# Every fifth broadcast of source indices on eight DMA engines instead of sixteen

## The chip, the cores and the metric

The kernel runs on one core of one Trainium2 chip. What counts is the device time of one execution in microseconds (us), as the median over several runs. A profile is one further execution, taken by the hardware profiler; its span runs from the first to the last instruction of the program.

Engines are named as in the profile: PE is the matrix engine, PEld its weight load, DVE the vector engine, ACT the scalar engine, POOL the GpSimd engine and SP the engine whose queue issues most of the plain transfers. Transfers are carried out by 16 DMA engines; a queue (q0, q1, q10 and so on) is a list of transfers that several DMA engines work on.

## What is computed

One layer of mean aggregation over a graph of 12,500 nodes and 800,000 edges, with 64 features a node:

```python
def reference(x, src, dst, deg_inv, w_self, w_neigh):
    N = x.shape[0]
    nsum = _segment_sum(x[src], dst, N)        # sum of x[src] over the edges of each dst
    h_neigh = nsum * deg_inv[:, None]
    return x @ w_self + h_neigh @ w_neigh
```

`src` and `dst` are random node numbers, so both the gather `x[src]` and the sum by `dst` are irregular.

## The kernel before

The irregular part is turned into matrix products. The edges are packed into 32-bit keys, sorted in runs of 6250 a partition, merged, and so brought into 8526 buckets. A bucket holds the edges whose destination lies in one block of 144 nodes and whose source lies in one block of 128 nodes; it has at most 128 edges (64 for each half of the destination block). All of this takes about the first half of the time.

For each bucket two lists of small numbers are left. One says which row of the destination block an edge goes to; it stays on the chip, transposed, in the tile `dlT`. The other says which of the 128 rows of the source block an edge takes. It is written to device memory as `sl`, one row of 128 numbers (bf16, 256 bytes) for a bucket.

The second half of the time is the loop in `nodes`, which walks through the buckets in tiles of 8. Its steps are:

- `one_hots` makes the operands for 28 buckets at a time, 305 times in all. Line 777, on SP's queue, fetches 28 rows of `sl`, that is 3584 numbers or 7168 bytes, and writes the same 7168 bytes to each of the 128 partitions of the tile `slb`: this is the broadcast that the change is about, 896 KB written for each. `slb` has three buffers. Line 779, on DVE, compares `slb` with the partition's own number and so makes the one-hot tile `ohs` (source row by edge; three buffers). Line 782, on DVE too, makes the one-hot tile `ohd` (edge by destination row; six buffers) from `dlT`.
- `gather` multiplies, on PE, each bucket's `ohs` with the rows of `x` of its source block (line 807, into the PSUM tile `ct`, 8 buckets each). ACT (line 817), and later sometimes DVE (line 815), copies `ct` to `xg`.
- `sums` multiplies `xg` with `ohd` and adds up in PSUM (line 863, tiles `acc`).
- Every 7 destination blocks, `finish` multiplies the sums with `w_neigh`, scales, adds the self term and stores the output.

The order of all this is written out by hand (`manual_schedule`), and each engine's queue runs in that order. `gather` asks `one_hots` for the next 28 buckets as soon as fewer than 44 buckets beyond its own 8 are ready (`AHEAD`), so one-hots are made a group or two ahead of the products. SP issues the broadcast of a group once DVE has read the `slb` buffer three groups back (line 779). Between the groups, DVE runs the merge of the second part of the keys (`merge_round`, lines 280 and 292) in the first part of the loop, and smaller work later. Other transfers in the loop are gathers and stores on POOL's queue (`v`, `lx`, `sl`, `out`), loads and stores on ACT's queue (`fo`, one store of merged rows `d`), and the fetching of instructions.

Of the kernel before, what the change touches and what calls it, by code (L numbers as in the profile page):

```python
# [335 lines left out]
class Kernel:  # L336
# [433 lines left out]
    def one_hots(self, pool):  # L770


        nc = self.nc
        for c in range(0, NBID, 28):
            b = pool.tile([128, 28 * 128], BF, name="slb", bufs=3)
            src = self.sl[c:c + 28]
            nc.sync.dma_start(b, bass.AP(tensor=src.tensor, offset=src.offset, ap=[[0, 128], [1, 28 * 128]]))
            s = pool.tile([128, 28, 128], FH, name="ohs", bufs=3)
            nc.vector.tensor_scalar(s.rearrange("p c s -> p (c s)"), b, self.pidx[:, :1], None, op0=OP.is_equal)  # L779
            d = pool.tile([128, 14, HN, 2], FH, name="ohd", bufs=6)  # L780
            ix = self.dlT[:, c:c + 28].rearrange("p (c t) -> p c t", t=2)[:, :, None, :].to_broadcast([128, 14, HN, 2])
            nc.vector.tensor_tensor(d, self.iota[:, None].to_broadcast([128, 14, HN, 2]), ix, op=OP.is_equal)  # L782
            yield [(s[:, j], d[:, j // 2, :, j % 2]) for j in range(28)]
# [376 lines left out]
```

## Time and profile before

| | |
|---|---|
| Time, median of 3 runs | 2198.76 us |
| The three runs | 2186.39, 2199.57, 2198.76 us |
| Time of the profiled execution | 2187.6 us |
| Span of the profiled execution | 2185.9 us |
| Busy in the span: PE, DVE, ACT, POOL | 1026.7, 1997.1, 1263.6, 648.6 us |
| Broadcasts on line 777 | 305, issued from 1098.1 to 2160.9 us |
| Moved by the DMA engines | 331.46 MB, of it 299.80 MB on q1 (SP's queue) |

The busy time of an engine is the time in which it executes; the profile also tells, for each stretch in which an engine was idle, what it had been waiting for. For the DMA engines the profile gives, by queue, the number of packets, the bytes, and the time that the packets took as a share of the time of all 16 engines; it does not say which engine carried which packet. The share and the bytes of a queue together give the pace of one engine while it works for that queue. All views can be cut to a stretch of the span, given in us from its start.

### The profile page before, as it was taken

Reading aid. Unit: us, or ns where it says so; the run is one execution under the profiler, and the core shown is the slowest. Engines: PE = TensorE matmul, PEld = TensorE weight load, DVE = VectorE, ACT = ScalarE, POOL = GpSimd, SP = SyncE. Lnnn points to the kernel's source line nnn. Section 1 sums busy time; section 2 is a strip of 40 time slices with the busy share of each in tenths; the row PEclk is TensorE's granted clock in tenths of the full one; section 3 lists DMA queues with packets and bytes.
Section 4 is the critical chain, followed back from the end, with each engine's and each line's share of the span. In section 5 each row is a group of like instructions: output and inputs, shape, how many; then the busy total and the mean of one; then the engine's idle time right before and its main releaser. Section 6 shows DMA issues by size and latency. Waiting matters only on the chain.

```text
span 2185.9 us, 59793 instructions
## 1 busy us (share of the span) xinstructions
PE 1026.7 (47%) x26089; PEld 885.7 (41%) x26089; DVE 1997.1 (91%) x2193; ACT 1263.6 (58%) x1743; POOL 648.6 (30%) x1016
## 2 busy tenths in 40 slices
PE   0050000000000000000068998999987989999888
PEld 0050000000000000000067887878776877788777
DVE  7899999999899599988999999999998988898887
ACT  6470000009700000062269999999998888898887
POOL 0000000000888888977771101011340110100110
PEclk9975555555555555555589999999999999999999
DMA  5140000001000000011177787777876787787785
GB/s 162 29 107 11 0 0 0 0 7 53 21 20 19 18 13 14 10 50 51 47 271 263 269 293 265 280 262 281 309 275 232 274 288 281 264 312 280 272 284 177
DMA packets 111471, 331.46 MB, mean 152 GB/s; under 512 B 57008, under 2 KB 65136, under 8 KB 110560
## 3 DMA queue, kind: packets, MB, share of 16 engines
q1 hardware_dynamic: 74127, 299.80, 37.0%
q0 software_dynamic: 14736, 18.99, 4.9%
q10 hardware_dynamic: 22337, 8.76, 1.8%
q8 instruction: 206, 3.38, 0.6%
q14 instruction: 65, 0.53, 0.1%
HBM read 308.39 MB, written 19.10 MB: 150 GB/s over the span
## 4 chain that ended last, share of the span: by engine, by line
PE 36%; DVE 33%; POOL 10%; issue 9%; ACT 8%; DMA 2%; ACTq 1%; another core or an unknown queue 0%; DVEq 0%; POOLq 0%; SPq 0%
PE ct L807 21%; PE acc L863 14%; DVE a L228 9%; DVE b L228 9%; POOL u L467 6%; DVE u L292 6%; ACT xg L817 3%; POOL pad L382 2%; ACT junka L448 2%; DVE u L324 2%; DMA v<-d,ix 1%; POOL v L625 1%; PE po L931 1%; DVE u L280 1%; ACT junk L604 1%
## 5 line engine op out<-in xcount | busy, mean ns | idle before, releaser
L817 ACT ACTIVATE xg<-ct 128x1024 f16<-128x1024 f32 (+1 forms) x994 | 939.1, 1091 | 99.2 <-PE ct L807 79.1
L807 PE MATMUL ct<-xh,ohs 128*128 128x128 f16 x8526 | 600.7, 221 | 58.0 <-issue 24.6
L807 PEld LDWEIGHTS <-ohs 128*128 128x128 f16 x8526 | 496.5, 99 | 104.7 <-issue 44.1
L467 POOL DMA_INDIRECT u<-d,ix x256 | 336.0, 1313 | 543.4 <-ACT junka L448 500.8
L292 DVE TENSOR_TENSOR u<-u 128x256 f32<-128x256 f32 (+47 forms) x494 | 452.8, 947 | 23.1 <-ACT u L276 15.7
L863 PE MATMUL acc<-ohd,xg 64*128 64x72 f16 x17052 | 410.1, 194 | 49.2 <-issue 35.1
L863 PEld LDWEIGHTS <-xg 64*128 64x128 f16 x17052 | 323.9, 94 | 124.6 <-issue 45.7
L779 DVE TENSOR_SCALAR ohs<-slb,pidx 128x3584 f16<-128x3584 bf16 x305 | 350.1, 1148 | 20.3 <-PE ct L807 17.1
L782 DVE TENSOR_TENSOR ohd<-iota,dlT 128x2016 f16<-128x2016 bf16 x305 | 365.8, 1199 | 0.0
L692 PE MATMUL tr<-idb,l 128*128 128x128 bf16 x68 | 9.0, 271 | 492.5 <-ACT l L686 487.6
L228 DVE TENSOR_TENSOR b<-a 128x106 f32<-128x106 f32 (+36 forms) x112 | 227.3, 2080 | 10.3 <-ACT a L231 9.3
L228 DVE TENSOR_TENSOR a<-b 128x106 f32<-128x106 f32 (+31 forms) x114 | 228.5, 2056 | 1.2
L276 ACT ACTIVATE u<-u 128x256 f32<-128x256 f32 (+15 forms) x94 | 47.3, 589 | 309.7 <-DVE u L280 308.3
L692 PEld LDWEIGHTS <-l 128*128 128x128 bf16 x68 | 5.6, 116 | 496.0 <-ACT l L686 491.4
L457 PE MATMUL stp<-idf,st 128*128 128x128 f32 x2 | 0.9, 446 | 420.4 <-DVE st L455 420.4
L939 POOL DMA_DIRECT2D out<-o x24 | 24.3, 1014 | 540.0 <-DVE o L938 470.6
L457 PEld LDWEIGHTS stp<-idf,st 128*128 128x128 f32 x2 | 0.4, 183 | 420.9 <-issue 420.9
L844 POOL DMA_INDIRECT lx<-xt,lxi x44 | 80.0, 1818 | 297.9 <-DVE lxi L842 181.0
L815 DVE CAST xg<-ct 128x1024 f16<-128x1024 f32 x75 | 91.6, 1222 | 58.1 <-PE ct L807 57.7
L231 ACT ACTIVATE a<-b 128x106 f32<-128x106 f32 (+12 forms) x20 | 13.5, 710 | 218.8 <-DVE b L228 195.2
L382 POOL MEMSET pad<- 128x89 f32 x594 | 114.6, 193 | 17.4
L625 POOL DMA_INDIRECT v<-d,ix x68 | 85.3, 1254 | 53.4 <-ACT ix L655 19.2
(134 smaller groups left out, 846.5 us busy)
## 6 DMA issues: line engine op xcount, KB each, us to landing
slb<-sl SPq DMA_DIRECT2D x305, 896.0 KB
u<-d,ix POOLq DMA_INDIRECT x256
xt<-xh SPq DMA_DIRECT2D x1, 3136.0 KB
own<-os SPq DMA_DIRECT2D x12, 256.0 KB
fo<-own ACTq DMA_DIRECT2D x24, 126.0 KB
out<-o POOLq DMA_DIRECT2D x24, 126.0 KB
rd<-dst SPq DMA_DIRECT2D x5, 521.0 KB
rs<-src SPq DMA_DIRECT2D x5, 521.0 KB
```

Source lines behind the costliest of these rows:

```text
L228: nc.vector.tensor_tensor(view(dst, lo + sh, [[st, g], [1, l]]), x, y, op=op)
L292: nc.vector.tensor_tensor(to, at(cur, ln + lo, n), at(cur, lo + k, n), op=op)
L382: self.nc.gpsimd.memset(self.pad, 0.0)
L467: nc.gpsimd.indirect_dma_start(out=u[:nr, p * w:(p + 1) * w], out_offset=None, in_=src, in_offset=bass.IndirectOffsetOnAxis(ap=self.start[ ...
L625: self.nc.gpsimd.indirect_dma_start(out=self.v[:, k].bitcast(F32), out_offset=None, in_=flat(self.d2[part], 128 * PITCH2[part]), in_offset ...
L779: nc.vector.tensor_scalar(s.rearrange("p c s -> p (c s)"), b, self.pidx[:, :1], None, op0=OP.is_equal)
L782: nc.vector.tensor_tensor(d, self.iota[:, None].to_broadcast([128, 14, HN, 2]), ix, op=OP.is_equal)
L807: nc.tensor.matmul(ct[:, i * 128:(i + 1) * 128], cols[i][0], self.xh[:, (b0 + i) % NB].rearrange("p a f -> p (a f)"), start=True, stop=True)
L815: nc.vector.tensor_copy(xg[:, :cnt * 128], ct[:, :cnt * 128])
L817: nc.scalar.activation(xg[:, :cnt * 128], ct[:, :cnt * 128], AF.Copy)
L844: nc.gpsimd.indirect_dma_start(out=x, out_offset=None, in_=self.xt, in_offset=bass.IndirectOffsetOnAxis(ap=ix.bitcast(U32), axis=0))
L863: nc.tensor.matmul(acc[h][:, db % OCT * HN:(db % OCT + 1) * HN], xg[r, i * 128:(i + 1) * 128], d[r], start=db % OCT == 0 and sb == 0, stop ...
```

## The change

The access pattern that describes the source of the broadcast gets another form. Before, it had two dimensions: 128 repeats of the same address (step 0), and 3584 consecutive numbers. In every fifth broadcast (groups 4, 9, 14 and so on to 304: 61 of 305) the 128 repeats are written as two dimensions, 8 repeats of 16 repeats, both with step 0. The numbers read, the tile written and the bytes moved are the same. The form is there so that the transfer goes out on eight DMA engines with 16 rows each, where the other 244 broadcasts go out on sixteen with 8 rows each.

```diff
@@ -774,7 +774,9 @@
         for c in range(0, NBID, 28):
             b = pool.tile([128, 28 * 128], BF, name="slb", bufs=3)
             src = self.sl[c:c + 28]
-            nc.sync.dma_start(b, bass.AP(tensor=src.tensor, offset=src.offset, ap=[[0, 128], [1, 28 * 128]]))
+
+            rows = [[0, 8], [0, 16]] if c // 28 % 5 == 4 else [[0, 128]]
+            nc.sync.dma_start(b, bass.AP(tensor=src.tensor, offset=src.offset, ap=rows + [[1, 28 * 128]]))
             s = pool.tile([128, 28, 128], FH, name="ohs", bufs=3)
```

Nothing else is changed.

## The prediction, made before the changed kernel was timed

> **What bounds the kernel now.** I read the page first, to see in which part of the span the changed line works and what is busy there.
>
> ```profile
> span 2185.9 us, 59793 instructions
> ...
> PE   0050000000000000000068998999987989999888
> ...
> DVE  7899999999899599988999999999998988898887
> ACT  6470000009700000062269999999998888898887
> ...
> DMA  5140000001000000011177787777876787787785
> ```
>
> Each digit is a fortieth of the span, 54.6 us. PE and the DMA engines work from the 21st slice on: that is the loop with the broadcasts, and everything before it doesn't touch line 777. In the loop three engines stand at 8 or 9 and the DMA engines at 7 or 8. Next come the same numbers for two stretches of the loop, one with DVE's merge and one after it (busy us of PE, PEld, DVE, ACT, POOL; then PE's clock, the busy share of the DMA engines, GB/s):
>
> ```profile
> 1110.00:1550.00 440.00, 409.51 (x10637) 352.04 (x10638) 428.16 (x467) 421.63 (x479) 72.95 (x45) 0.98 0.78 276
> 1550.00:2150.00 600.00, 538.66 (x14447) 468.66 (x14447) 532.07 (x648) 519.24 (x594) 95.18 (x76) 0.99 0.78 278
> ```
>
> In the first stretch DVE is idle for 440 - 428.16 = 11.8 us, so whatever holds DVE up there is lost nearly in full. In the second it is idle for 600 - 532.07 = 67.9 us, and PE is the busiest. Who waits for whom in the loop (1110 to 2160 us: total us, times, longest), and the chain that ended last, cut to the same stretch:
>
> ```profile
> PE acc L863 <- issue: 35.1, 36, 2.7
> PE ct L807 <- issue: 24.6, 25, 3.1
> ...
> PE ct L807 <- DVE ohs L779: 0.2, 1, 0.2
> ...
> DVE ohs L779 <- DMA slb<-sl: 0.6, 1, 0.6
> ...
> SPq L777 <- DVE ohs L779: 877.1, 292, 11.1
> ```
>
> ```profile
> 1548.09 6.30 DMA d<-u
> 1562.22 3.14 DMA v<-d,ix
> ```
>
> DVE waited for a broadcast once, for 0.6 us. The DMA pieces among the longest of the chain are a store and a gather, not a broadcast. SP spent 877.1 us waiting for DVE to give an `slb` buffer back, so its queue is not late either. **The broadcast is hidden now, and the question is how much room hides it.**
>
> **Room in time.** A broadcast is issued when DVE has read the buffer three groups back, and is needed when DVE comes to its own group. Here is one in the first stretch, with the first of all at 1098.12:
>
> ```profile
> 1098.12 0.32 SPq L777 DMA_DIRECT2D slb<-sl  x1
> 1102.62 1.25 DVE L779 TENSOR_SCALAR ohs<-slb,pidx 128x3584 f16<-128x3584 bf16 x1 [1.46 <-DMA slb<-sl]
> ...
> 1501.13 1.15 DVE L779 TENSOR_SCALAR ohs<-slb,pidx 128x3584 f16<-128x3584 bf16 x1
> ...
> 1502.31 0.32 SPq L777 DMA_DIRECT2D slb<-sl  x1
> ...
> 1504.96 1.15 DVE L779 TENSOR_SCALAR ohs<-slb,pidx 128x3584 f16<-128x3584 bf16 x1
> ...
> 1507.21 1.15 DVE L779 TENSOR_SCALAR ohs<-slb,pidx 128x3584 f16<-128x3584 bf16 x1
> ...
> 1511.03 1.15 DVE L779 TENSOR_SCALAR ohs<-slb,pidx 128x3584 f16<-128x3584 bf16 x1
> ```
>
> The buffer read at 1501.13 is free at 1502.28, the issue follows at 1502.31, and the third `ohs` after it starts at 1511.03: 8.72 us from issue to need. The first broadcast found idle DMA engines and DVE waiting, and took 1102.62 - 1098.12 = 4.50 us.
>
> **Room in load.** The DMA engines from 1110 to 2150 us (1040 us), by queue: packets, MB, share of 16 engines; and the issues of line 777 in it:
>
> ```profile
> q1 hardware_dynamic: 42723, 272.26, 69.4%
> q0 software_dynamic: 4616, 7.75, 5.6%
> q10 hardware_dynamic: 16664, 4.48, 1.9%
> q8 instruction: 195, 3.19, 1.2%
> q14 instruction: 34, 0.28, 0.1%
> ...
> slb<-sl SPq DMA_DIRECT2D x296, 896.0 KB
> ```
>
> q1 is all but the broadcasts: 296 x 896 KB is 271.6 MB. One engine at work on q1 moves 272.26 MB / (0.694 x 16 x 1040 us) = 23.6 GB/s. A sixteenth of 896 KB is 57,344 bytes, so a broadcast holds each engine for 2.43 us; 4.50 - 2.43 = 2.07 us is left for issue and landing. Broadcasts come 1040 / 296 = 3.51 us apart. The other queues add 5.6 + 1.9 + 1.2 + 0.1 = 8.8% to each engine, if spread evenly.
>
> **The change, part by part.** Nothing is removed: 305 broadcasts, the same bytes, the same instructions on PE, DVE and ACT in the same hand-written order. SP issues 61 of the 305 with a source of one more dimension; should that lengthen an issue of 0.32 us severalfold, it comes out of SP's 877.1 us, and behind it on SP's queue stand only further broadcasts. What moves is load. Eight engines carry 16 rows where they carried 8, the other eight none.
>
> *The broadcast itself.* No row of before shows one on eight engines, so its row is priced from both sides. Low end: an engine keeps the pace of q1, 16 rows take 4.86 us, and the transfer 2.07 + 4.86 = 6.93 us, which is 1.79 us less than the 8.72 us that it has. High ends: the paces that other patterns of this kernel reach in the same stretch, q10 with 4.48 MB / (0.019 x 16 x 1040 us) = 14.2 GB/s, a row 1.66 times as long, and q0 with 7.75 MB / (0.056 x 16 x 1040 us) = 8.3 GB/s, 2.8 times. I take the low end, q1, because it is the same queue, the same 7168 bytes a row and the same tile; q10 and q0 carry short rows (under 300 bytes a packet on q10).
>
> *What then comes late.* If the broadcast finds another whole one of 2.43 us ahead of it, it lands 2.43 - 1.79 = 0.64 us after its need. That can't be more than some 25 of the 61 times in the first stretch (440 of 1040 us), so 16 us; the 36 later ones, 23 us, fit in DVE's 67.9 us of idle time. Nothing at all is the other end, as DVE waited only once for a broadcast. I take 5 us, a third of the way. A gain is left to the rivals.
>
> *The broadcast behind it.* It is issued 3.51 us later on average, finds the low eight engines busy for 4.86 - 3.51 = 1.35 us more, and lands 4.50 + 1.35 = 5.85 us after issue: hidden by the same 8.72 us.
>
> *Load.* In five broadcasts the low eight engines carry 4 x 8 + 16 = 48 rows for 40, the others 32. Their share goes to 69.4 x 48 / 40 + 8.8 = 92.1%, the others' to 64.3%. Below 100% the loop need not stretch. With a row f times as long in the eight-engine broadcast, the low eight are full at (32 + 16 f) / 40 x 69.4 + 8.8 = 100, that is **f = 1.29**. That is the point from which the forecast turns.
>
> **Sum.** 2187.6 us for the profiled execution (1.7 us more than its span) + 5 = 2192.6. That execution lies 11 us under the median of the runs, so against the median I say 2198.76 + 5 = 2204 us. A measurement of this kernel tells a change from none at about 1%, 22 us.
>
> **Rivals.**
>
> *The eight engines slow one another (slower).* Sixteen rows on one engine are another set of partitions than the eight rows of before, and engines that wrote side by side may now write to the same place by turns. From f = 1.29 on, the low eight engines become the bound of the loop. At f = 1.66 (q10's pace) they need 110.5% of the loop's time, +109 us; at f = 2 they need 119.8%, +206 us; at q0's 2.8, +446 us. I put this case half way between the first two, +157, at 2356 us, with 2307 to 2405 for its own range. For it speaks that the pace of an engine is no constant here (23.6, 14.2 and 8.3 GB/s on three queues) and that 92.1% leaves little room; against it, that the row and the queue are those of the 23.6.
>
> [...]
>
> *The form is not seen (no change).* Two dimensions of step 0 are the same walk as one, and if the transfer is still dealt out in sixteen shares, all rows stay as they are: 2199 us. Nothing in the profile speaks against it, as no issue there has such a source.
>
> [...]
>
> *The other eight engines are relieved (faster).* They fall from 78.2% to 64.3%. PE waited 35.1 + 24.6 = 59.7 us for its own instructions ("issue"), and q8 fetched them in 195 packets. If those ride on the relieved engines and a third of the wait goes, that is -20 us, 2179. Against it: they may as well ride on the engines that get fuller.
>
> **Chances and range.** Forecast 0.44, slowing engines 0.43, form not seen 0.08, relief 0.05. The slow case is nearly as likely as the forecast because f = 1.29 lies only a little above the end that I take, 1, and both other ends, 1.66 and 2.8, lie beyond it. Faster by over 1% has 0.03 (the larger half of relief); slower by over 1% has 0.43 and another 0.03 for a forecast whose queues back up at 92.1%; within 1% the rest, 0.51. The forecast's own range is 2186 (the fastest run of before) to 2215 (16 us late in full). To leave out no more than 2 in 10, the range has to reach over most of the slow case: 2186 to 2400, which leaves out some 0.12 above and 0.04 below. q0's end lies above it; scattered gathers are the poorest likeness of a broadcast.
>
> **What would show it.** Forecast: the loop's DMA share stays at 0.78, q1's share near 69%, and DVE's wait for `slb` on line 779 grows from 0.6 us to tens of us at most, by lots under 2 us. Slowing engines: q1's pace falls under 23.6 GB/s at the same packets and bytes, the broadcasts take over in the chain, DVE's wait for `slb` goes over 100 us and PE waits for `ohs` and not only for "issue". Form not seen: both rows as before. Relief: PE's 59.7 us of "issue" shrink. The forecast is wrong if a row on eight engines takes over 1.29 times what it does on sixteen, or if the other queues' packets sit on the low eight engines alone: these would then stand at 83.3 + 17.6 = 100.9%.

## The result, and the profile after

The changed kernel takes 2416.79 us (median of 4 runs, 2409.69 to 2434.85) where the kernel before takes 2198.28 us (4 runs, 2186.39 to 2199.57): 1.101 times as long, 95% interval 1.096 to 1.106. That is 218 us slower, and 17 us above the upper end of the range.

The profiled execution took 2434.85 us. Its page, in the rows that were read first of before (the span, then busy tenths in 40 slices of 60.8 us):

```profile
span 2433.1 us, 59792 instructions
...
PE   0130000000000000006878877878868788878787
...
DVE  6999999998996999797878887877867677667666
ACT  5450000086100104325878877878857667767666
...
PEclk9965555555555555557898988989889888888889
DMA  6040000010000001117888888788878878888876
```

The loop with the broadcasts still begins at 1098 us, and all that is lost is lost in it. No engine has taken over: PE, DVE and ACT are all less busy in the loop, and the clock that PE was granted has fallen too. The two stretches of the loop (busy us of PE, PEld, DVE, ACT, POOL; clock; DMA share; GB/s):

```profile
1110.00:1550.00 440.00, 354.63 (x8643) 308.21 (x8640) 351.39 (x389) 348.69 (x393) 40.95 (x39) 0.90 0.82 223
1550.00:2150.00 600.00, 478.03 (x11731) 416.58 (x11731) 446.37 (x542) 436.79 (x505) 84.62 (x67) 0.89 0.83 227
```

The DMA engines are busier than before (0.82 for 0.78) and move less (223 GB/s for 276). The queue of the broadcasts, 1110 to 2405 us:

```profile
q1 hardware_dynamic: 42574, 274.33, 75.8%
...
slb<-sl SPq DMA_DIRECT2D x299, 896.0 KB
```

One engine at work on q1 now moves 274.33 MB / (0.758 x 16 x 1295 us) = 17.5 GB/s, where it moved 23.6: the average row takes 1.35 times as long. That the form goes out on eight engines is read from the packets of q1: at the same bytes over the whole span (299.80 MB) they fall from 74,127 to 73,639, by 488, and it is the packets of 4 bytes that are fewer, 8 for each of the 61 broadcasts, where the first broadcast, on sixteen, has 16. Lines of the changed kernel stand two further down than before, so that 779 has become 781. Here is one broadcast on eight engines, in the timeline (start, us, engine, line, op; in brackets the idle time before and what ended it):

```profile
1490.31 0.60 SPq L779 DMA_DIRECT2D slb<-sl  x1
```

```profile
1502.88 1.15 DVE L781 TENSOR_SCALAR ohs<-slb,pidx 128x3584 f16<-128x3584 bf16 x1 [3.64 <-DMA slb<-sl]
...
1504.76 0.57 PE L865 MATMUL acc<-ohd,xg 64*128 64x72 f16 x13 [6.09 <-issue]
```

DVE was free 12.57 - 3.64 = 8.93 us after the issue, about the 8.72 us of room that was forecast, and got its row 3.64 us late. Two microseconds on, PE goes on after standing for 6.09 us, and not for that row: it had stopped at 1498.67, 0.57 us before DVE began to wait. The same in total, from the view of waits (total us, times, longest), 1110 to 2405 us:

```profile
DVE ohs L781 <- DMA slb<-sl: 196.4, 61, 7.7
...
PE acc L865 <- issue: 109.7, 43, 6.1
...
PE ct L809 <- issue: 78.4, 28, 6.3
...
PE ct L809 <- DVE ohs L781: 11.7, 11, 3.8
```

DVE now waits 61 times for a broadcast, 3.2 us each; 52 of these waits, 189 of the 196 us, are for one of the 60 broadcasts on eight engines in this stretch. The chain that ended last agrees: in this stretch broadcasts are 17.4% of it and "issue" is 16.0%, where "issue" was 10.9% before and broadcasts had no part in it. But PE's waits for `ohs`, which DVE makes from them, are only 11.7 us. What PE waits for is "issue", its own instructions: 188.1 us in 71 waits, where it was 59.7 us in 61. PE's busy time, for the same 26,089 matmuls, went from 1026.7 to 1102.2 us. **Longer waits for instructions (128 us) and the same work at a lower clock (75.5 us) make 204 of the 247 us by which the span grew.** Whether DVE's lateness or PE's own instructions come first is what the experiments had to settle.

### The profile page after: what moved, and what is told of

The parts are those of the page before. It is cut to its first block, busy times and chain, and to the rows that moved or that the text cites. A ratio compares the mean times of both kernels' runs of the same rounds, so it can differ in the third digit from the quotient of the medians.

```text
span 2433.1 us, 59792 instructions
## 1 busy us (share of the span) xinstructions
PE 1102.2 (45%) x26089; PEld 956.7 (39%) x26089; DVE 2002.4 (82%) x2193; ACT 1269.3 (52%) x1743; POOL 623.2 (26%) x1016
## 3 DMA queue, kind: packets, MB, share of 16 engines
q1 hardware_dynamic: 73639, 299.80, 43.8%
## 4 chain that ended last, share of the span: by engine, by line
DVE 27%; PE 26%; POOL 16%; DMA 14%; issue 13%; ACT 3%; ACTq 1%; DVEq 0%; SPq 0%; POOLq 0%
PE ct L809 15%; POOL u L467 12%; DMA slb<-sl 10%; PE acc L865 9%; DVE a L228 9%; DVE b L228 9%; POOL pad L382 4%; DVE ohs L781 2%; DVE ohd L784 2%; DMA lk<-lt 1%; DVE u L292 1%; DMA fo<-own 1%; ACT xg L819 1%; POOL v L625 1%; PE po L933 1%
## 5 line engine op out<-in xcount | busy, mean ns | idle before, releaser
L809 PE MATMUL ct<-xh,ohs 128*128 128x128 f16 x8526 | 654.6, 234 | 134.0 <-issue 79.0
L809 PEld LDWEIGHTS <-ohs 128*128 128x128 f16 x8526 | 545.1, 105 | 182.8 <-issue 105.7
L865 PE MATMUL acc<-ohd,xg 64*128 64x72 f16 x17052 | 433.6, 202 | 132.5 <-issue 109.7
L467 POOL DMA_INDIRECT u<-d,ix x256 | 323.3, 1263 | 542.8 <-ACT junka L448 500.4
L865 PEld LDWEIGHTS <-xg 64*128 64x128 f16 x17052 | 348.1, 99 | 210.5 <-issue 140.2
L846 POOL DMA_INDIRECT lx<-xt,lxi x44 | 72.2, 1642 | 420.0 <-PE ct L809 201.3
L382 POOL MEMSET pad<- 128x89 f32 x594 | 110.9, 187 | 17.5
```

The costliest lines, as they stand in the source:

```text
L382: self.nc.gpsimd.memset(self.pad, 0.0)
L467: nc.gpsimd.indirect_dma_start(out=u[:nr, p * w:(p + 1) * w], out_offset=None, in_=src, in_offset=bass.IndirectOffsetOnAxis(ap=self.start[ ...
L809: nc.tensor.matmul(ct[:, i * 128:(i + 1) * 128], cols[i][0], self.xh[:, (b0 + i) % NB].rearrange("p a f -> p (a f)"), start=True, stop=True)
L846: nc.gpsimd.indirect_dma_start(out=x, out_offset=None, in_=self.xt, in_offset=bass.IndirectOffsetOnAxis(ap=ix.bitcast(U32), axis=0))
L865: nc.tensor.matmul(acc[h][:, db % OCT * HN:(db % OCT + 1) * HN], xg[r, i * 128:(i + 1) * 128], d[r], start=db % OCT == 0 and sb == 0, stop ...
```

## Experiments

In the texts on record VectorE is DVE, TensorE is PE, SyncE is SP. The letters stand for theories; what each says is told with it. In "A" the rows of the eight engines take turns, in "L" what they cost is DVE's lateness, in "F" what they cost is PE's own instructions.

**1. How long does such a broadcast take by itself?** A kernel of its own sends 7168 bytes to 128 partitions, one transfer after another, each waited for by DVE, in several forms:

```
("sixteen",  [(0, 128, [[0, 128]])]),
("eight",    [(0, 128, [[0, 8], [0, 16]])]),
("pieces",   [(p, 32, [[0, 8], [0, 4]]) for p in range(0, 128, 32)]),
("straight", [(0, 128, [[0, 16], [0, 8]])]),
("halves",   [(p, 64, [[0, 8], [0, 8]]) for p in range(0, 128, 64)]),
("four",     [(0, 128, [[0, 4], [0, 32]])]),
("two",      [(0, 128, [[0, 2], [0, 64]])]),
...
```

> A small kernel that leaves the layer out and stores zeros. It copies one row of 7168 bytes from device memory to partitions of a tile, in eight written forms, six times each, one at a time: DVE reads the tile before the next copy is issued. sixteen: 128 repeats (16 engines, 8 rows each). eight: 8x16 (the changed form). pieces: four copies of 32 partitions, each 8x4 (eight engines, 16 rows each in all). straight: 16x8 (16 engines, 8 rows each, written as 8 in a row). halves: two copies of 64 partitions, each 8x8. four: 4x32. two: 2x64. Theory A, engines that write to partitions 32 apart take turns (row 0.27 us alone, 0.54 us in pairs; 2.1 us for issue and landing): sixteen 4.3 us from issue to DVE's read, eight 10.8, pieces 6.5 to 7.5, straight 6.5, halves 10.8, four 19.5, two 19.5. Theory B, an engine keeps 0.27 us a row whatever it writes to: sixteen 4.3, eight 6.5, pieces 6.5 to 7.5, straight 4.3, halves 6.5, four 10.8, two 19.5.

In its timeline, DVE's instruction behind a transfer of each form (in brackets how long DVE waited for it):

```profile
44.98 0.17 DVE L46 TENSOR_SCALAR ssixteen<-sixteen 128x8 f32<-128x8 f32 x1 [4.45 <-DMA sixteen<-x]
...
83.99 0.17 DVE L46 TENSOR_SCALAR seight<-eight 128x8 f32<-128x8 f32 x1 [10.50 <-DMA eight<-x]
...
134.38 0.17 DVE L46 TENSOR_SCALAR spieces<-pieces 128x8 f32<-128x8 f32 x1 [7.05 <-DMA pieces<-x]
...
176.81 0.17 DVE L46 TENSOR_SCALAR sstraight<-straight 128x8 f32<-128x8 f32 x1 [6.41 <-DMA straight<-x]
...
353.57 0.17 DVE L46 TENSOR_SCALAR sfour<-four 128x8 f32<-128x8 f32 x1 [15.97 <-DMA four<-x]
...
411.50 0.17 DVE L46 TENSOR_SCALAR stwo<-two 128x8 f32<-128x8 f32 x1 [20.30 <-DMA two<-x]
```

Each form was sent six times, the first time while the form before was still under way. The other times lie within 0.7 us of these lines, but "pieces" spreads from 6.95 to 8.69 us and "four" from 15.5 to 17.5.

Eight engines take 10.50 us, and 6.93 had been forecast. With the forecast's 2.07 us for issue and landing, 16 rows take 8.43 us, 0.53 each; on sixteen engines 8 rows take 2.38 us, 0.30 each: f = 1.77. The form "straight" tells why. It is written for sixteen engines, 8 rows each, as "sixteen" is (in the loop of experiment 2 its queue has 157 packets per MB, as before), but takes 6.41 us for 4.45. What is different must be which partitions are written side by side. No view shows that, so it is taken from the forms as they are written: with 16 (or 8) consecutive partitions for an engine, some engines begin 32 partitions apart. "Pieces", in which eight engines share 32 consecutive partitions, 4 rows each, take 7 to 8.7 us for the same bytes on the same number of engines. "Halves", in which eight engines share 64 partitions, 8 rows each, take 10.5 to 10.8 us, as theory A had said. The records of the single packets show it row by row: the median row takes 272 ns in "sixteen", "pieces" and "two", and 544, 533 and 540 ns in "eight", "straight" and "halves". So engines slow one another by where they write. "Four" was expected at 19.5 us and took 15.97; that part of the theory is too simple.

By the forms as written, no two engines of "pieces" and "two" begin 32 partitions apart, and the median row takes 272 ns; in "eight", "straight" and "halves" some do, and it takes twice as long. The starts of "pieces" lie 4 to 28 apart and those of "two" 64, so at these distances the median row is as short as in "sixteen". In "four" the starts lie 32, 64 and 96 apart, and the median row takes 361 ns. Over a whole transfer the price is under 2: by the sum above a row takes 0.53 us in "eight", 0.54 in "straight" and 0.43 in "four", 1.5 to 1.8 times the 0.30 of "sixteen".

**2. Is it the eight engines, or the partitions?** Every fifth broadcast as four transfers of 32 partitions, eight engines with 4 rows each, so that the eight still carry 16 rows; and every fifth on sixteen engines in the form "straight".

```diff
+            if c // 28 % 5 == 4:
+                for p in range(0, 128, 32):
+                    nc.sync.dma_start(b[p:p + 32], bass.AP(tensor=src.tensor, offset=src.offset,
+                                                           ap=[[0, 8], [0, 4], [1, 28 * 128]]))
```

```diff
+            rows = [[0, 16], [0, 8]] if c // 28 % 5 == 4 else [[0, 128]]
```

> Every fifth broadcast goes out as four copies of 32 partitions, each written 8x4, so that eight engines carry 16 rows each as in the changed kernel, but at any moment to partitions of their own. Theory A (engines that write to partitions 32 apart take turns): the row keeps its 0.27 us, the low eight engines stand near 92%, and the time is within 1% of the kernel before, 2195 to 2215 us. Theory B (twice the rows on eight engines is too much by itself, through the queue behind them or the instruction fetch that rides on them): as slow as the changed kernel, 2400 to 2430 us. In between would mean that both have a part.

> Every fifth broadcast is written 16x8: sixteen engines as before, 8 rows each, but 8 partitions in a row. [...] Theory B: the same as before in share and in time, 2199 us.

2259.46 us, 1.026 [1.020, 1.031], and 2263.98 us, 1.028 [1.022, 1.035]. The same 16 rows on the same number of engines cost 55 us in place of 218 when they go out so that, as written, no two engines begin 32 partitions apart; that lies between the two theories, so both the turns and the sixteen rows have a part. And sixteen engines in the slow order cost 60 us, although this broadcast fits in its room (6.41 us by itself, for 8.72):

```profile
PE acc L865 <- issue: 65.7, 54, 3.7
PE ct L809 <- issue: 49.3, 30, 4.2
...
DVE ohs L781 <- DMA slb<-sl: 10.5, 14, 2.4
```

DVE waits 10.5 us in all, PE 115 us for its instructions. Theory B had given 2199 us, and 60 us are lost beside a wait of 10.5: something other than DVE's lateness costs time.

**3. Does the cost begin where the engines are full?** Every tenth, and every twentieth broadcast on eight engines.

```diff
+            rows = [[0, 8], [0, 16]] if c // 28 % 10 == 9 else [[0, 128]]
```

> Every tenth broadcast on eight engines instead of every fifth (30 of 305). If each such broadcast costs its own lateness, the extra time is half of the 218 us, so 2300 to 2310 us. If it is the load of the low eight engines that binds (by the prediction's sum 99.0% of the loop's time at twice the row time, 119.8% at every fifth), most of it goes: 2205 to 2250 us.

> Every twentieth broadcast on eight engines (15 of 305). Every tenth cost 125 us, 4.2 us each, and every fifth 218 us, 3.6 us each. If each costs its own lateness, whatever the load: 15 x 4.2 = 63 us, 2255 to 2275 us. If there is a share of idle time that takes up the first ones (67.9 us of DVE's in the second half of the loop), less than half of that: 2200 to 2230 us.

2329.82 us, 1.058 [1.053, 1.064], and 2267.06 us, 1.031 [1.025, 1.037]. For 15, 30 and 61 broadcasts the loss against the runs beside them is 61, 125 and 218 us: 4.1, 4.2 and 3.6 us each. Every tenth cost more than either theory gave, every twentieth what was forecast for a fixed price each. With f = 1.77 the low eight engines, if every such broadcast goes to the same eight as the forecast has it (no view shows which), would need (152 + 28.3) / 160 x 69.4 + 8.8 = 87% of the loop of before in the first case, 96% in the second and 113% in the third. The load theory gives nothing, nothing and 139 us; it falls. In the loop rows are slower than alone: with every twentieth on eight engines a row takes 335 ns on average, and 303 before. If all that extra time lay on the low eight engines, they would stand at 96%, still not full, and 61 us are lost. The loss needs no full engine. Whether the eight are nearly full in the changed kernel itself stays open; at least eight packets are under way in 91% of its loop, for 78% before.

**4. Is it that DVE gets its row late?** If so, a fourth `slb` buffer hides it. To make room, `ohd` gets 5 buffers for 6 and `xg` 5 for 7, in the kernel before as well.

```diff
-            b = pool.tile([128, 28 * 128], BF, name="slb", bufs=3)
+            b = pool.tile([128, 28 * 128], BF, name="slb", bufs=4)
```

> The kernel before with four slb buffers instead of three; to make room, ohd has five buffers for six and xg five for seven. It is the control of the next run. A broadcast is hardly ever waited for in the kernel before, so no theory expects a gain: within 1% of before, unless the smaller ohd and xg cost something.

> The changed kernel with the same four slb buffers (and five each of ohd and xg). A broadcast may then take about 3.5 us longer before DVE waits: some 12.2 us instead of 8.7, against a landing measured at 11 to 13.5 us after issue in the changed kernel. Theory A1 (the time is lost because every eight-engine broadcast lands some 3.6 us after DVE wants it): most of the 218 us goes, at most 60 us over its control. Theory A2 (the low eight engines are full, or the instruction fetch is held up behind the slow rows, whatever DVE does): DVE's wait for slb shrinks, but the kernel stays at least 120 us over its control.

> Every fifth broadcast as four copies of 32 partitions, 8x4 each, with four slb buffers (five each of ohd and xg): eight engines carry 16 rows, no two on one place, and a broadcast has about 12 us. If the 2.6% of that form with three buffers was DVE waiting for slb (38.5 us up to 2200 us of the span), it falls to the level of the run with four copies on sixteen engines, +0.5 to +1.5%. If it was the instruction fetch behind fuller engines, it stays at +2% or more.

> Every tenth broadcast on eight engines, with four buffers of broadcast rows. By the rows of before and twice the time of a row, the low eight engines then carry 104 rows' worth for 80 in ten broadcasts, 1.3 x 69.4 + 8.8 = 99% of the loop's time: just not full. Theory L (what cost 125 us in the kernel with every tenth and three buffers was that VectorE got each such broadcast 3.8 us late): the fourth buffer covers it, VectorE's wait falls from 109 us to under 30 and the time from 2330 us to 2195 to 2230. Theory F (while one engine of a pair writes 16 rows, whatever else is on these engines waits, TensorE's instructions above all; so each such broadcast costs its part, waited for or not): VectorE's wait falls too, but the time stays above 2290 us, and TensorE's idle time put down to issue is over 110 us (73 us in before with four buffers, 199 us in the changed kernel with four).

Before with these buffers: 2201.27 us, 0.998 [0.995, 1.001]. The changed kernel: 2433.53 us, 1.103 [1.097, 1.109], no better than with three. The four transfers of 32: 2261.05 us, 1.029 [1.026, 1.032], and every tenth: 2322.83 us, 1.056 [1.052, 1.060], both as before. The waits of the last, 1110 to 2290 us:

```profile
PE acc L865 <- issue: 81.5, 37, 5.9
...
PE ct L809 <- issue: 52.0, 26, 6.4
...
DVE ohs L781 <- DMA slb<-sl: 13.1, 8, 2.9
```

DVE's wait fell from 119.6 to 13.1 us and the time did not move; PE's wait for its instructions stayed at 133.5 us (135.5 with three buffers). DVE now waits for PE instead: its waits for an `ohs` buffer that PE still reads go from 24.4 to 83.4 us. Lateness is real, but taking it away gives nothing back, because PE's stops remain.

**5. What does lateness alone cost?** Before, with something ahead of every fifth broadcast that holds SP's queue: two numbers go to the buffer, to device memory and back, once or three times. All rows go out on sixteen engines.

```diff
+            if c // 28 % 5 == 4:
+                nc.sync.dma_start(b[:1, :2], src[:1, :2])
+                for _ in range(3):
+                    nc.sync.dma_start(self.slow, b[:1, :2])
+                    nc.sync.dma_start(b[:1, :2], self.slow)
             nc.sync.dma_start(b, bass.AP(tensor=src.tensor, offset=src.offset, ap=[[0, 128], [1, 28 * 128]]))
```

> The kernel before, all broadcasts on sixteen engines. Ahead of every fifth broadcast SP sends two numbers into its buffer, from there to device memory and back, each waiting for the one before, so that the broadcast is issued some 6 us after its buffer is free, and the one behind it late too. The DMA engines get next to no more work. Theory L (what costs the 218 us is that DVE gets every fifth broadcast some 3.6 us late): about as slow as the changed kernel, at least 2330 us. Theory F (the rows that block the low eight engines also hold up PE's instructions, and a late broadcast by itself is mostly taken up by the one-hots made ahead): PE's waits for its own instructions stay near the 60 to 73 us of before, and the time is under 2290 us.

> As the run before with the two numbers sent on ahead of every fifth broadcast, but to and fro three times: at the 1.1 us a step measured there the broadcast is issued some 7.5 us after its buffer is free and lands about as late as the eight-engine one does (12 to 13 us), with all rows on sixteen engines at their normal pace. DVE's wait for slb should come near the 196 us of the changed kernel (the weaker delay gave 48 us of wait and 39 us of time). Theory L (DVE's lateness is the cause): 2350 to 2420 us, with PE's waits for its own instructions near 85 us as in the weaker run. Theory F (the held-up instruction fetch and the slower PE clock that follows are most of it): DVE waits as long, but the time stays under 2320 us.

> The kernel of the longer delay (every fifth broadcast issued some 7.5 us later, all on sixteen engines), with four buffers of broadcast rows in place of three, five of doubled one-hots in place of six and five of gathered rows in place of seven, as in the other kernels with four buffers. Theory L (lateness is all: what a broadcast costs is the time that VectorE stands before it): the fourth buffer lets SyncE issue about 20 us sooner, VectorE's wait for the broadcast falls from 288 us to under 30, and the time from 2445 us to 2195 to 2230. With it falls lateness as the reason for the changed kernel with four buffers (2434 us, VectorE's wait 52 us): there it must be the full engines, on which TensorE's own instructions wait (its idle time put down to issue was 199 us), and here that idle time stays under 90 us. Theory K (the time is lost elsewhere, in the order of buffers or in SyncE's queue, whatever VectorE waits for): it stays above 2380 us as the changed kernel did, with VectorE's wait small.

Once: 2237.86 us, 1.020 [1.016, 1.023]; the delay, from the first of the small transfers to the broadcast, was 3.9 us in the median and not the 6 us wanted, too short to tell. Three times: the delay was 8.4 us and the time 2445.09 us, 1.111 [1.106, 1.116], as slow as the change. So theory F was wrong where it said that a late broadcast by itself is mostly taken up. With four buffers: 2391.66 us, 1.086 [1.079, 1.093]; the wait stayed at 227.5 us, presumably because the broadcasts behind the trip stand in the same queue and the fourth buffer can't let them by. That last run tests neither theory. But the waits of the one with three trips, 1110 to 2412 us, show what a loss by lateness looks like:

```profile
DVE ohs L784 <- DMA slb<-sl: 280.8, 82, 9.2
...
PE ct L812 <- DVE ohs L784: 144.3, 64, 6.9
...
PE ct L812 <- issue: 6.5, 8, 2.1
...
PE acc L868 <- issue: 3.8, 6, 1.6
```

PE waits for DVE, 144.3 us for `ohs`, and for its own instructions only 10.3 us; presumably they come while it waits for `ohs`. In the changed kernel it is the other way round, 11.7 and 188.1. Late broadcasts could cost as much as the change did; in the change the loss goes by another way.

**6. Does a transfer that nobody waits for cost it too?** Before with four `slb` buffers, and behind every fifth broadcast one more, of half the width, into a tile that nobody reads, once on eight engines and once on sixteen (4 buffers of `xg`).

```diff
+            if c // 28 % 5 == 4:
+                x = pool.tile([128, 14 * 128], BF, name="spare", bufs=1)
+                nc.sync.dma_start(x, bass.AP(tensor=src.tensor, offset=src.offset,
+                                             ap=[[0, 8], [0, 16]] + [[1, 14 * 128]]))    # or [[0, 128]]
```

> Before with four buffers of broadcast rows, and behind every fifth broadcast one more transfer in the eight-engine form, of half the width (448 KB, 16 rows of 3584 bytes an engine), into a tile that nobody reads; four buffers of gathered rows. All 305 broadcasts are on sixteen engines. At twice the time of a row the low eight engines stand at (40 + 16) / 40 x 69.4 + 8.8 = 106% of the loop's time of before. Theory F (what full engines delay costs, TensorE's instructions above all, whatever VectorE waits for): 2250 to 2330 us, TensorE's idle time put down to issue over 110 us, VectorE's wait for broadcasts under 50 us. Theory L (only a late broadcast costs): within 1.5% of before, up to 2232 us, as nobody waits for the extra transfer and the broadcasts behind it have four buffers of room.

> The same extra transfer of 448 KB behind every fifth broadcast, written in the form that goes out on sixteen engines, 8 rows each. All engines stand at 44 / 40 x 69.4 + 8.8 = 85%. Both theories: 2195 to 2225 us; it shows what the extra bytes, the extra issue and the buffers cost, beside the run with the eight-engine form. Above 2240 us the extra bytes themselves would be the cost and that run would tell little of the form.

On eight: 2316.96 us, 1.052 [1.048, 1.056]; on sixteen: 2240.25 us, 1.018 [1.014, 1.022], 15 us above the range given for it and at the bound of 2240 us from which the extra bytes themselves count. Waits of the one on eight, 1110 to 2297 us, and of the one on sixteen, 1110 to 2208 us:

```profile
PE acc L867 <- issue: 90.7, 62, 5.4
...
PE ct L811 <- issue: 51.6, 33, 3.8
...
DVE ohs L783 <- DMA slb<-sl: 1.1, 1, 1.1
```

```profile
PE acc L867 <- issue: 48.2, 46, 3.2
...
PE ct L811 <- issue: 42.2, 31, 3.0
```

All broadcasts come as they did before, and DVE waits for one once, 1.1 us. PE's wait for its instructions is 142 us with the eight-engine form and 90 us without it, and the time 77 us apart at the same bytes; the 52 us of PE's wait and 30 us more of its busy time make up this difference. **Rows in the eight-engine form cost time through PE's instructions even when no engine waits for them.**

**7. Is it only that one broadcast becomes four?** Every fifth as four quarters of the columns, each on sixteen engines.

```diff
+            for q in range(0, 28, 28 if c // 28 % 5 != 4 else 7):
+                w = 28 if c // 28 % 5 != 4 else 7
+                part = self.sl[c + q:c + q + w]
+                nc.sync.dma_start(b[:, q * 128:(q + w) * 128], bass.AP(tensor=part.tensor, offset=part.offset,
+                                                                       ap=[[0, 128], [1, w * 128]]))
```

> Every fifth broadcast goes out as four copies of 128 partitions and a quarter of the columns each, all on sixteen engines: as many issues as in the run with four pieces of 32 partitions, but no load moved and no place shared. If the 2.6% of that run comes from the four issues (SP, semaphores), this one is as slow, 2250 to 2265 us. If it comes from the 16 rows on eight engines, this one is within 1% of before, 2190 to 2215 us.

2227.96 us, 1.011 [1.007, 1.015], between the two forecasts. Four issues, here with four times as many rows of a quarter of the length, cost 22 us, so the issues alone don't make the 55 us of the four transfers of 32 partitions.

All of it side by side: the time, the loss against the runs of before on the same chip, PE's wait for "issue" in the loop (up to 28 us before the end of the span), PE's busy time, and DVE's wait for broadcasts, in us.

| kernel | time | loss | PE for its instructions | PE busy | DVE for broadcasts |
|---|---|---|---|---|---|
| before (profiled once) | 2198 | | 60 | 1026.7 | 1 |
| before, four buffers | 2201 | -5 | 71 | 1025.7 | 1 |
| four quarters of columns | 2228 | 22 | 100 | 1028.3 | 1 |
| extra transfer on sixteen | 2240 | 41 | 90 | 1036.6 | 0 |
| every fifth in 32s | 2259 | 55 | 98 | 1046.8 | 41 |
| the same, four buffers | 2261 | 62 | 100 | 1040.9 | 2 |
| every fifth 16 x 8 | 2264 | 60 | 115 | 1035.5 | 11 |
| every twentieth on eight | 2267 | 61 | 101 | 1041.7 | 55 |
| extra transfer on eight | 2317 | 117 | 142 | 1066.8 | 1 |
| every tenth on eight, four buffers | 2323 | 123 | 134 | 1076.0 | 13 |
| every tenth on eight | 2330 | 125 | 136 | 1068.8 | 120 |
| changed kernel | 2417 | 218 | 188 | 1102.2 | 196 |
| the same, four buffers | 2434 | 227 | 199 | 1096.6 | 52 |
| *delay, one trip* | 2238 | 39 | 84 | 1031.3 | 48 |
| *delay, three trips* | 2445 | 246 | 10 | 1086.9 | 281 |
| *the same, four buffers* | 2392 | 192 | 16 | 1088.4 | 228 |

Leaving out the three delays, the loss follows the third column: each us that PE stands longer for its instructions goes with 0.5 to 1.5 us of loss in the rows that lose less than 100 us, and with 1.4 to 1.7 in the five that lose more. It does not follow the last column. What the loss has beyond 1 us for each us of PE's wait is mostly the busy time: PE does the same work more slowly after it has stood. None of these is faster than the kernel before.

That PE stands for instructions is the profile's "issue", which only means that nothing it shows was waited for. The records of the single packets tie it to the fetch on q8 (206 packets of 16 KB, one for each 253 of PE's matmuls and weight loads). Of PE's stops of over 0.5 us in the loop that are put down to "issue", all 44 of before and 58 of the changed kernel's 61 end 1.1 to 1.8 us after a packet of q8 has landed. By chance it would be about one in ten: 197 packets with 0.7 us each in 1295 us. These are the sums over all of PE's idle times of over 0.5 us that end so:

```
kernel                     times  us     longest us
before                     47     57.7   3.1
extra transfer on sixteen  66     90.6   3.3
extra transfer on eight    74     139.6  5.4
changed kernel             64     188.4  6.3
changed, four buffers      67     209.0  9.6
```

They account for the column to within 10 us. The same records tie the long stops to the broadcasts on eight engines. In the changed kernel such a broadcast is under way, from issue to landing, for 58% of the loop; the 46 stops behind a packet that started in this time last 3.5 us on average, the other 12 last 1.8 us. With every twentieth on eight engines (17% of the loop) these are 17 stops of 2.9 us and 36 of 1.3 us, and all 8 stops of over 3.2 us are among the 17.

## Why the prediction was wrong

- **The broadcast itself: this is the step that failed.** It took the low end, f = 1, "because it is the same queue, the same 7168 bytes a row and the same tile". The experiment with one transfer at a time gives f = 1.77, so the transfer takes 10.50 us, more than the 8.72 us of room. The high ends, 1.66 and 2.8, held it. In the changed kernel the slowest quarter of the rows begins at 532 ns, where it began at 275 ns before. What the step didn't ask is which partitions the engines write at the same time; the nearest row in bytes and queue was not the nearest in that.
- **A second step failed with it: the forecast had no term for PE's own instructions.** It read their 59.7 us of waits and priced what relieved engines might do to them, but put what fuller engines do at nothing. They became 188.1 us, and with the slower clock that followed they make 204 of the 247 us.
- **Room in time** held: 8.72 us were forecast and DVE was ready 8.93 us after the issue. In the broadcast shown, with 12.6 us to landing, 3.6 us late follow. "What then comes late" put 5 us in place of 196.4, through f and through what a slower broadcast does to the rows behind it. It took DVE's wait for the loss; the runs with four buffers show that the wait can go and the loss stay.
- **The broadcast behind it** was to land after 5.85 us; by the packet records it lands after 11.5 us in the median, hidden by its own later need.
- **Load.** The shares were to stay at 0.78 and 69%; they are 0.82 and 75.8% at fewer bytes per us. At f = 1.77 in a fifth of the rows the average row would be 1.15 times as long, and it is 1.35: a third of all rows take over 400 ns (8% before), more than the fifth that goes out on eight engines, so other rows are slowed too. No view gives a single engine's share.
- **SP's longer issue**, 0.60 us for 0.32, came out of its waiting time as said.
- **The rival "the eight engines slow one another"** had the cause and at f = 2 nearly the size, +206 us for +218. But that price was right by chance. No run shows its f = 2: one such transfer by itself gives 1.77. It let the eight engines become full from f = 1.29 on; the loss is there at 87 to 96% load, grows with the number of such broadcasts, and at the measured 1.77 its sum gives 139 us. Of its signs, q1's slower pace, DVE's wait over 100 us and the broadcasts in the chain came; PE waited 11.7 us for `ohs`, and "issue" stayed its main wait.
- **The rival "relieved"** looked at the right row, PE's 59.7 us of "issue", with the wrong sign: they became 188.1. Its own counter-argument, that the fetches may ride on the engines that get fuller, was the way in which most of the time went, as far as the packets show it, and stood without a price.
- **The form not seen** fell: an issue took 0.60 us for 0.32, and each such broadcast has 8 packets fewer.

The chain, then: engines that, as the form is written, begin 32 partitions apart slow one another (a median row of 544 ns for 272); the rows of such a broadcast hold them for longer (8.43 us for 2.38, by the sum above); a 16 KB packet of PE's instructions that falls in this time comes later (the stops that end behind one last 3.5 us on average and 6.3 us at most, where before all such stops lasted 1.2 and 3.1); PE stands, and everything behind it in the hand-written order stands too; and after a stop PE runs for a while at the lower clock (0.90 and 0.89 for 0.98 and 0.99).

The clock's own records in the traces show this last step. In the loop of before PE had half its clock in 8 stretches, 30.7 us in all; in the changed kernel in 53, 290.1 us, and 7 of the 8 and all of the 53 begin within 7 us of a stop of over 0.5 us. In the run with three trips, where PE stops for `ohs` and not for instructions, it is 47 stretches and 266.2 us, each behind a stop too, and PE's busy time grows by 60 us. So the clock falls whatever PE stops for.

Most of the fetches are hidden: of 198 packets in the loop before 47 are followed by a stop, and of 197 after 64. But the rest is not small: PE's waits for instructions are 59.7 us before and 188.1 us after. The stretches at half the clock last 3.41 us or a multiple of it (9 times 3.41 us in all before, 85 times after); 21 of the 53 follow stops that were all shorter than 3.4 us, so a stop need not last as long as such a stretch.

What stays open: which DMA engines carry the fetches, and why one is held up by that much; no view tells engines apart, and a fetched packet itself takes hardly longer (1.01 us before, 1.17 us after, on average). No run took PE's stops away and left the change, so their part is shown by their growth beside the loss, and by the loss that stays when lateness goes. And how much the lateness would cost if the fetches were not held up can't be read from these runs; the delays say up to 0.9 us for each us that DVE waits, so it might cost nearly as much.

## What to carry to other kernels

A transfer's price is not its bytes, its queue and its number of engines alone (here 6.41 us for 4.45 with all three the same): ask which partitions the engines write at the same moment, and time one such transfer by itself before you price it by its likeness. When transfers get slower, look first at what else uses the DMA engines, the instruction fetch of the busiest engine above all: a wait put down to "issue" that grows (59.7 to 188.1 us here) may be a transfer too, and the packets of the fetch's queue show whether the wait ends behind one. And a wait that grows by as much as the time (DVE's 196 us here) is not yet the cause, and neither is its share of the chain: see whether the engine behind it waits for it, and hide it to find out.

## What was not expected of the hardware

- Sixteen engines with 8 rows each take 4.45 us for 896 KB in the form of before, and 6.41 us when, as written, each has 8 consecutive partitions; 2 engines with 64 rows take 20.3 us and 4 with 32 rows 16.0, so here twice the engines brought little.
- A source with one more repeat dimension took SP longer to issue: 0.54 us on sixteen engines and 0.60 us on eight, for 0.33 us.
- A transfer that no engine waits for, 448 KB in every five broadcasts, cost 41 us in 2200 on sixteen engines and 117 us on eight.
